# A recurrent transformer and a gated MLP on one core: the last quarter of the first filler chunk moved behind Wo, and row sums spread over two segments

## The chip, the core and the metric

The kernel runs on one core of a Trainium2 chip. The metric is the device time in microseconds; three runs of the kernel before took 1677.53, 1683.88 and 1685.84 us, median 1683.88.

## What is computed

`_A_ref` is a recurrent transformer over 64 segments of 32 rows; each sees 8 memory rows ahead of its own, and the first 8 rows of its output are the memory of the next. `_B_ref` is a gated MLP with a 2048x2048 spatial gate.

```python
def _A_ref(x, mem0, Wq, Wk, Wv, Wo, seg_len):      # Dm 512, 32 heads of 128, M 8, seg 32
    for s in range(n_seg):                         # 64
        h = jnp.concatenate([mem, xs], axis=1)     # 40 rows
        q, k, v = (einsum('btd,dhe->bhte', h, W) for W in (Wq, Wk, Wv))
        p = _softmax(where(mask, q k^T * scale, -1e9))
        o = jnp.einsum('bhte,hed->btd', p v, Wo)
        mem = o[:, :M, :].copy()
        outs.append(o[:, M:, :])
...
def _B_ref(x, w_in, w_sp, b_sp, w_out):            # x 2048x512, w_in 512x1376
    z = _gelu(x w_in);  z1 = z[..., :688];  z2 = _layernorm(z[..., 688:])
    return (z1 * (w_sp z2 + b_sp)) w_out
x = x + _A_ref(_layernorm(x), ...)
x = x + _B_ref(_layernorm(x), ...)
x = x + _A_ref(_layernorm(x), ...)
x = x + _B_ref(_layernorm(x), ...)
```

The sketch writes the einsums of the reference in a short form.

## The kernel before

The program is A, B, A, B: `a_block` (segments), then `b_block` (gMLP), twice. Instructions of TensorE (PE), VectorE (DVE) and ScalarE (ACT) run in the order in which the program writes them (`ORDERED`, `manual_schedule`, L667), in b_block those of SyncE too; around the seam between two blocks a planner still merges the two written orders. GpSimd (POOL) and, in a_block, SyncE are placed by the planner. Each engine works off its queue in order, so an instruction that waits holds up all behind it.

**A segment** (`segment`, L852) takes a little over 10 us. PE projects the 40 rows with Wq, Wk, Wv (groups of four matmuls, one for each 32-row strip of the array, `mm_chunk` L679), computes scores for the two halves r of the heads (`scores`, L899 for the memory part), softmax sums (L921, L930) and the values (`pv`, L938 and L941). ACT scales the scores (L904), DVE adds the mask into E (L907), ACT inverts the sums by Ln and Exp (`memory_out` L955 and L956; all rows L1013 and L1016). DVE writes the normalised heads to uT (L957 for the rows that become memory, L960 and L963 for others). Wo follows in two forms: `wo_pairs` (L755) takes the first `WO_PAIR` heads into the bank px, 2 matmuls of 256 columns a head, `wo_rest` (L762) the others into a strip of psO, 4 matmuls of 128 columns. ACT copies half of px (`odd`, L1011), DVE adds both halves (`fold`, L838), adds psO (memT, L843) and transposes into hT (L844): the memory with which the next segment's first projection (psQ) starts. This is a serial chain through all 64 segments.

**Fillers.** While a segment waits for itself, PE takes pieces of other work by `fill`, which runs a generator to its next `yield`: `b_units` (L718) projects the last 8 rows of each segment of the next 128-row block, six chunks of 16 matmuls, two chunks a segment; `y_part` (L778) applies Wo to such rows of a finished group. The first chunk of a segment was cut into 4, 8 and 4 matmuls: the first 4 before `sums_memory(0)`, the 8 and the last 4 (`fill(2)`) before `sums_memory(1)`; the second chunk, whole, stands behind Wo and covers the memory chain. Both take the PSUM bank accA; px, psm and psV take the bank accB. What ACT does for a chunk is put into `copies` and run at two places (`run(copies)`, which takes the last appended first): behind `memory_out(1)`, ahead of `odd`, and behind the second chunk.

**Row sums.** A finished 128-row block of A's output gets its residual and its layernorm for the gMLP while later segments run. In one segment each, from `tail` to `tail`: loads on SP (`y_load` L204, to tiles y_x and y_o), the sum on POOL (`y_add` L211, in `spare1`), `y_stats` on DVE (bn_stats L134 on 512 columns, in `spare2`, ahead of the fold), the reciprocal root on ACT (`_rstd_act`, Ln L111 and Exp L112, by `copies`), the norm on DVE (`y_norm` L221) and its store. `rows.apply` and `_stats` do the same for the input of later blocks in the first A block.

**The seam.** Behind segment 63 one row (block 11) is finished by hand: its load was issued in segment 63's `spare1` into `rowsB`, the sum is on DVE; then come the last segment's Wo (pw, L1129), its copy (o_end, L1132), two adds on DVE (L1135), stores of them (L1137 on POOL, L1139 on SP) and the load of ACT's gelu table (L106). `b_block` then runs `project(tt)` for 16 row blocks: 16 groups of matmuls into pz (L268, two PSUM buffers), a gelu on ACT (L269), statistics on DVE (L272). Rows 12 to 15 are still due: their loads are on POOL (L205, L207; row 12 in a y_x and a y_o tile, row 15 in a half of wspL), their sums and statistics (`late_sum`) stand behind projects 1, 2 and 3 on DVE, the reciprocal roots on DVE (`norms`), and `late_norm` stores them on POOL. Transposed loads of pairs of row blocks (`load_rows`, L167, on SP) bring them to PE: projects 12 and 13 need rows 12 and 13. Then the gate runs on PE (pg, L369).

Of the kernel before, what the change touches and what calls it, by code (L numbers as in the profile page):

```python
# [8 lines left out]
F32 = mybir.dt.float32  # L9
# [5 lines left out]
P = 128  # L15
DM = 512
# [9 lines left out]
LN_EXP_SET = 6  # L26
GELU_SET = 11
WO_LOW = (4, 4, 4, 3)
WO_PAIR = 14
OLD_SIZES = (H * P, 8 * DH, H * 32, H * 32)  # L30
ORDERED = {mybir.EngineType.PE, mybir.EngineType.DVE, mybir.EngineType.Activation}

# [77 lines left out]
def _rstd_act(nc, out, var, c):  # L110
    nc.scalar.activation(out=out, in_=var, func=ACT.Ln, bias=c["eps_t"][:], scale=1.0)  # L111
    nc.scalar.activation(out=out, in_=out, func=ACT.Exp, scale=-0.5)  # L112
# [19 lines left out]
def _stats(nc, pool, x_tile, MV_out_slot):  # L132
    st = pool.tile([P, nc.vector.BN_STATS_DIM], F32, name="bnst")
    nc.vector.bn_stats(out=st[:], in_=x_tile)  # L134
    nc.vector.bn_aggr(out=MV_out_slot, in_=st[:])


class _Front:
# [496 lines left out]
def a_block(tc, c, rows, front, MV_in, RS_in, MV_out, RS_out, ahead, wo, S, first):  # L635
    nc = tc.nc
    NSEG = S // SEG
    NB = S // P
# [3 lines left out]
    with ExitStack() as ctx:  # L642
# [69 lines left out]
        copies, turns, adds = [], [], []  # L712

        def run(todo):
            while todo:
                todo.pop(0)()

        def b_units(tb, early=False):  # L718
            bs = blk_state[tb]

            for k, j in enumerate((0, 2, 1, 3, 4, 5) if early else (4, 5, 0, 2, 1, 3)):
                ps = (accB if early and k in (1, 3) else accA).tile([P, 512], F32, name="psb")[:]
                for kts in (((0,), (1, 2), (3,)), ((0, 1, 2, 3),))[k % 2]:
                    mm_chunk(ps, lambda kt, cg: bs["hB"][:, kt, :],
                             lambda kt, cg: qk_rhs(w, j, kt, cg) if j < 4 and early else cols_rhs(w, j, kt, cg), kts)
                    if kts[-1] != KT - 1:
                        yield

                def out(k=k, j=j, ps=ps):
                    if j >= 4:  # L730
                        nc.scalar.copy(bs["VB"][:, :, j - 4, :], ps.rearrange("p (i e) -> p i e", i=4))
                        if j == 5 and early:
                            ahead.regroup(bs["VB"], bs["VX"])
                        elif j == 5:
                            store_v(bs)
                        return
                    r = rowsB[:, k % 2, :]
                    nc.scalar.copy(r, ps)
                    t = bs[("QTB", "KTB")[j // 2]][:, j % 2]
                    if early:  # L740
                        turns.append(lambda: nc.vector.transpose(out=t.rearrange("p a b -> p (a b)"), in_=r))
                    else:
                        nc.sync.dma_start_transpose(out=t.rearrange("p (i g) k -> p i (g k)", g=4), in_=r.rearrange("t (i e) -> t i e", i=4))

                copies.append(out)
                yield

        def wo_pairs(px, lhs):  # L750

# [26 lines left out]
        def y_part(G, q, last=False):  # L778

            groups = [oBs[G][:, :, 32 * g:32 * g + 32] for g in range(4)]  # L780
            if last:
                parts = [[(groups[g], 8 * q + k) for g in range(3)] + [(groups[q], 24 + k)] for k in range(8)]
            else:
                parts = [[(groups[g], 8 * q + k) for g in range(4)] for k in range(8)]
            pwB = accA.tile([P, DM], F32, name="pwB")
            for k, _ in enumerate(wo_last(parts, pwB)):
                if k in (0, 2, 3):
                    yield

            def add(lo, n, src):  # L790
                nc.vector.tensor_tensor(out=yB[G][lo:lo + n, :], in0=pwB[src:src + n, :], in1=yB[G][lo:lo + n, :], op=ALU.add)

            def out():
                n = 96 if last else P
                if q == 0:
                    yB[G] = wk.tile([P, DM], F32, name="yB", bufs=1)
                    nc.vector.tensor_copy(yB[G][0:n, :], pwB[0:n, :])
                else:
                    add(0, n, 0)
                if last:  # L800
                    if q == 2:
                        store_last(G, 0, 64, nc.sync)
                    add(32 * q, 32, 96)
                    if q == 2:
                        store_last(G, 64, 96, nc.sync)
                elif q == 3 and G < NB // 4 - 2:
                    stores.append(lambda: store_last(G, 0, P, nc.sync))
                elif q == 3:
                    store_last(G, 0, P, nc.sync)

            adds.append(out)
            yield

        def y_stats(tb):
            rows.y_stats(tb, MV_out[:, tb, :])
            copies.append(lambda: _rstd_act(nc, RS_out[:, tb:tb + 1], MV_out[:, tb, 1:2], c))

        def y_norm(tb, store):
            rows.y_norm(tb, MV_out[:, tb, 0:1], RS_out[:, tb:tb + 1], store)
# [32 lines left out]
        def segment(s, fill, spare1, spare2, tail):  # L852
# [143 lines left out]
            memory_out(0)  # L996
            spare1()
            if not (first and s == 0):
                fill(2)
            sums_memory(1)  # L1000
            pv(1)
            psT = att.tile([P, 2, 512], F32, name="psT")
# [55 lines left out]
        for s in range(NSEG):  # L1058
            tb, j4 = s // 4, s % 4
            if first and s == 0:  # L1060
                more = values(units)
            elif j4 > 0 and tb == NB - 1:
                more = y_part(tb // 4, j4 - 1, last=True)
            elif j4 == (3 if tb < NB - 1 else 0) and tb > 3:
                more = y_part(tb // 4 - 1, tb % 4)
            elif j4 == (first and tb == 0):
                more = b_units(tb + 1)
            if j4 == 1 and tb + 2 < NB:
                rows.load(tb + 2, first, nc.sync)

            def spare1():
                if ys:
                    rows.y_add(ys[0], first, nc.gpsimd, nc.sync)
                elif stores:
                    last = yB[max(yB)][:, 0:1]
                    nc.vector.tensor_copy(last, last)
                    run(stores)
                if j4 == 3 and tb + 2 < NB:
                    rows.apply(tb + 2, MV_in, RS_in, first=first)
                if s == NSEG - 2:  # L1080
                    nc.vector.memset(front.w_in_sb[:, 2, FH - 1:FH + 1], 0.0)
                    front.load_w(2)
                if s == NSEG - 1:
                    nc.vector.memset(rowsB[:, 0, 0:1], 0.0)
                    rows.y_load(due[0], first, nc.sync, rows.pool.tile([P, DM], F32, name="y_x")[:],
                                rowsB[:].rearrange("p a n -> p (a n)").bitcast(F32))()

            def spare2():
                if first and s == 0:
                    rows.apply(1, MV_in, RS_in, first=True)  # L1090
                if first and s == 8:
                    c["cast_bsp"] = c["load_bsp"]()
                if first and s == 12:
                    c["cast_bsp"]()
                if ys:
                    y_stats(ys[0])
                if j4 == 2 and tb + 2 < NB and first:
                    _stats(nc, rows.pool, rows.xs[tb + 2], MV_in[:, tb + 2, :])
                    copies.append(lambda: _rstd_act(nc, RS_in[:, tb + 2:tb + 3], MV_in[:, tb + 2, 1:2], c))

            def tail():
                if j4 == 1 + (first and tb == 0) and tb + 1 < NB:
                    spread_v(blk_state[tb + 1])
                if tb == NB - 1:
                    if j4 != 2:
                        front.load_w(j4)
                    if j4 > 0:
                        front.load_rows(j4 - 1)
                if ys:
                    y_norm(ys.pop(0), nc.sync)  # L1110
                if j4 == 0 and tb > 7 and (tb % 4 == 0 or tb == NB - 1):
                    due.extend(range(tb // 4 * 4 - 8, tb // 4 * 4 - 4) if tb < NB - 1 else range(NB - 8, NB - 4))

                if due and (j4 != 3 or tb + 2 >= NB) and s < NSEG - 1:
                    ys.append(due.pop(0))
                    rows.y_load(ys[0], first, nc.sync)()

            segment(s, lambda n=1: [next(more, None) for _ in range(n)], spare1, spare2, tail)
        assert not ys and due == [NB - 5]
        rows.y_add(due[0], first, nc.vector, nc.sync)  # L1120
        y_stats(due[0])
        run(copies)
        y_norm(due[0], nc.sync)
        ends = (uT[NSEG % 2], oBs[NB // 4 - 1][:, :, 96:128])
        pw = accB.tile([P, 512], F32, name="pw")
        for i in range(H // 2):
# [50 lines left out]
```

## Time and profile before

| what | value |
|---|---|
| median of 3 runs | 1683.88 us |
| the profiled execution | 1684.06 us |
| its span | 1682.4 us |
| PE busy | 1605.9 us, 95% |
| DVE, ACT, POOL busy | 1185.9, 1093.7, 270.3 us |
| granted TensorE clock, mean | 0.996 of full speed |

A line of a timeline gives the start in us, the duration, engine and line, the operation, the tile written and those read, the shapes and the number of instructions put together; in brackets stand the idle time ahead of it on its engine and who ended it. PEld is a weight load of PE, beside its matmuls. POOLq and SPq are DMA issues of those engines. In the waits, a line names the engine, the tile and line that waited, what it waited for, the sum, the number and the longest. All times count from the start of the span.

### The profile page before, as it was taken

The numbers are of one execution on the slowest core, as the hardware profiler recorded it, in microseconds if no ns is written. First come the engines' busy times: TensorE is split into PE (matmuls) and PEld (weight loads), VectorE is DVE, ScalarE is ACT, GpSimd is POOL, SyncE is SP. The second block draws the span as 40 slices with busy tenths as digits, with TensorE's granted clock in tenths as the row PEclk, the third lists the DMA queues.
The fourth block names the chain that finished last, engine by engine and source line by source line (L and its number), as shares of the span: only waits on it lengthen the run. The fifth ranks groups of instructions, "written<-read, shape, count | busy, mean of one in ns | idle before, by whom it ended". The sixth has DMA issues, their size and how long they took to land.

```text
span 1682.4 us, 89162 instructions
## 1 busy us (share of the span) xinstructions
PE 1605.9 (95%) x40146; PEld 934.0 (56%) x40146; DVE 1185.9 (70%) x2848; ACT 1093.7 (65%) x2276; POOL 270.3 (16%) x548
## 2 busy tenths in 40 slices
PE   0999999998999999999999999999999999999999
PEld 0555555554555555556645555555555555655565
DVE  1777777777777787785357777777787778777722
ACT  0677777776777777662037777777777777776500
POOL 5111111111111121220011111111121112112100
PEclk9999999999999999999999999999999999999999
DMA  9222121113312333276972112112252125235697
GB/s 353 90 48 42 41 41 42 42 41 86 73 42 43 81 87 72 68 178 144 196 192 43 44 44 47 49 45 45 51 129 48 44 51 133 56 61 155 144 199 164
DMA packets 270822, 149.45 MB, mean 89 GB/s; under 512 B 199769, under 2 KB 243409, under 8 KB 270441
## 3 DMA queue, kind: packets, MB, share of 16 engines
q1 hardware_dynamic: 262584, 117.23, 31.0%
q0 software_dynamic: 7856, 26.51, 4.7%
q8 instruction: 315, 5.16, 1.3%
q14 instruction: 67, 0.54, 0.1%
HBM read 59.68 MB, written 37.19 MB: 58 GB/s over the span
## 4 chain that ended last, share of the span: by engine, by line
PE 86%; DVE 5%; DMA 5%; ACT 2%; issue 1%; POOL 1%; SPq 0%; DVEq 0%; POOLq 0%; ACTq 0%
PE psQ L679 14%; PE psK L679 13%; PE psb L679 10%; PE psO L762 6%; PE psm L679 6%; PE pg L369 6%; PE px L755 6%; PE psV L679 6%; PE pz L268 4%; PE pwB L774 3%; PE psO L921 2%; PE psO L938 2%; PE psT L930 2%; PE py L412 2%; PE psS L895 1%; DMA Wk_sb<-in_A_Wk_dram 1%
## 5 line engine op out<-in xcount | busy, mean ns | idle before, releaser
L679 PEld LDWEIGHTS <-hT 128*32 128x32 bf16 x12288 | 313.5, 97 | 353.1 <-DVE hT L844 71.4
L872 DVE STREAM_TRANSPOSE QQ<-rows 128x512 bf16<-128x512 bf16 x256 | 181.0, 707 | 28.4 <-ACT rows L869 22.2
L872 DVE STREAM_TRANSPOSE KA<-rows 128x512 bf16<-128x512 bf16 x256 | 179.8, 702 | 27.5 <-ACT rows L869 21.1
L869 ACT CAST rows<-psQ 128x512 bf16<-128x512 f32 x256 | 148.1, 587 | 45.4 <-PE psQ L679 45.2
L957 DVE TENSOR_TENSOR uT<-psO,Rm 128x128 bf16<-128x128 f32 x256 | 74.5, 291 | 137.0 <-ACT Rm L956 136.1
L679 PE MATMUL psQ<-Wq_sb,hT 128*32 128x512 bf16 x2048 | 136.2, 385 | 21.3 <-DVE hT L844 15.2
L960 DVE TENSOR_TENSOR uT<-psO,Rt 128x384 bf16<-128x384 f32 x256 | 141.0, 551 | 20.3 <-ACT Rt L1016 16.7
L369 PE MATMUL pg<-z,wspT 128*128 128x344 bf16 x1024 | 154.4, 309 | 0.0
L762 PE MATMUL psO<-Wo_high,uT 128*32 128x128 bf16 x8704 | 148.6, 220 | 2.4 <-issue 2.1
L1016 ACT ACTIVATE Rt<-Rt 128x512 f32<-128x512 f32 x256 | 147.2, 622 | 4.1
L762 PEld LDWEIGHTS <-uT 128*32 128x32 bf16 x9216 | 143.8, 97 | 5.6 <-issue 4.4
L904 ACT ACTIVATE S<-psS 128x224 bf16<-128x224 f32 x256 | 91.4, 357 | 80.8 <-PE psS L899 80.8
L679 PE MATMUL psQ<-Wk_sb,hT 128*32 128x512 bf16 x2048 | 134.8, 382 | 0.0
L679 PE MATMUL psm<-Wq_sb,hT 128*32 128x512 bf16 x2048 | 134.2, 381 | 0.0
L679 PE MATMUL psK<-Wk_sb,hT 128*32 128x512 bf16 x2048 | 133.6, 379 | 0.0
L679 PE MATMUL psK<-Wv_sb,hT 128*32 128x512 bf16 x2048 | 133.4, 379 | 0.0
L1013 ACT ACTIVATE Rt<-psT 128x1024 f32<-128x1024 f32 x128 | 131.0, 1023 | 3.1
L679 PE MATMUL psV<-Wv_sb,hT 128*32 128x512 bf16 x2048 | 132.8, 378 | 0.0
L369 PEld LDWEIGHTS <-wspT 128*128 128x128 bf16 x1024 | 100.1, 98 | 53.4 <-DMA wspT<-in_B_w_sp_dram 0.3
L955 ACT ACTIVATE Rm<-psO 128x128 f32<-128x128 f32 x256 | 71.0, 277 | 84.4 <-PE psO L941 70.8
L755 PE MATMUL px<-Wo,uT 128*32 128x256 bf16 x3584 | 121.7, 275 | 0.5 <-DVE uT L957 0.5
L831 POOL COPY KX<-front 128x128 bf16<-128x128 bf16 x128 | 68.3, 550 | 321.1 <-PE psS L899 249.3
(171 smaller groups left out, 2758.4 us busy)
## 6 DMA issues: line engine op xcount, KB each, us to landing
o_d<-o_sb SPq DMA_DIRECT2D x126, 64.0 KB
vb_d<-front SPq DMA_DIRECT2D x30, 256.0 KB
VX<-vb_d SPq DMA_DIRECT2D x120, 64.0 KB
ln_x<-xd SPq DMA_DIRECT2D x26, 256.0 KB
y_o<-o_d SPq DMA_DIRECT2D x22, 256.0 KB
xd<-y_o SPq DMA_DIRECT2D x22, 256.0 KB
y_x<-xd SPq DMA_DIRECT2D x22, 256.0 KB
Wq_sb<-in_A_Wq_dram POOLq DMA_DIRECT2D x8, 512.0 KB, 9.2
```

The costliest lines, as they stand in the source:

```text
L369: nc.tensor.matmul(pg[t][:, k, 0:344], lhsT=wsp[t][:, st, :], rhs=z(st, 344 * k, 344 * k + 344), start=(st == 0), stop=(st == NT - 1))
L679: return [nc.tensor.matmul(ps[32 * cg:32 * cg + 32, :], lhsT=lhs(kt, cg), rhs=rhs(kt, cg), start=(kt == 0), stop=(kt == KT - 1), tile_posi ...
L755: nc.tensor.matmul(px[at:at + 32, 0:256], lhsT=lhs[:, h, :], rhs=wo_rhs(h, slice(k, 4, 2)), start=(h < 2), stop=(h >= WO_PAIR - 2), tile_p ...
L762: nc.tensor.matmul(pw[32 * cg:32 * cg + 32, :], lhsT=lhs[:, h, :], rhs=wo_rhs(h, cg), start=False, stop=(h == H - 1), tile_position=(0, 32 ...
L869: return r, mms, nc.scalar.copy(r[:], ps)
L872: nc.vector.transpose(out=QQ[:, j % 2, :, 0:32] if j < 2 else KA[:, j % 2], in_=r[:])
L904: return nc.scalar.activation(out=S[:, r], in_=psS[:, r, 0:224], func=ACT.Exp, scale=scale)
L955: nc.scalar.activation(out=rm, in_=psO[r][:, :, 320:384], func=ACT.Ln)
L957: nc.vector.tensor_tensor(out=hview(uT_cur[:], r, 24, 32), in0=oview(r, 0, 8), in1=rm.rearrange("p g (n q) -> p g n q", q=8), op=ALU.mult)
L960: nc.vector.tensor_tensor(out=hview(uT_nxt[:], r, 0, 24), in0=oview(r, 8, 32), in1=rview(r, 0, 24), op=ALU.mult)
L1013: nc.scalar.activation(out=Rt[:], in_=psT[:], func=ACT.Ln)
L1016: nc.scalar.activation(out=rt, in_=rt, func=ACT.Exp, scale=-1.0)
```

## The change

Two heads of Wo move from `wo_pairs` to `wo_rest` (14 to 12). The last quarter of a segment's first filler chunk (in `y_part` likewise) moves from before `sums_memory(1)` to behind Wo, ahead of the second chunk; the second chunk takes accB, px's bank; the first chunk's copy is no longer ahead of `odd`, and both copies run behind the second chunk. A row sum takes two segments: load in the `tail` of one, the sum on POOL in the next one's `spare1`, statistics in two halves of 256 columns in `spare1` and `spare2` of the one after it, norm and the next load in its `tail`. The input's statistics of the first A block are halved in the same way. In the last segments a load may be issued for row 11 into `rowsB`, in segment 63's `tail`, so that behind the loop rows 10 and 11 both get statistics, reciprocal roots and norms, where only row 11 did.

```diff
-WO_PAIR = 14
+WO_PAIR = 12
...
+def _half_stats(nc, st, x_tile, k, MV_out_slot):
+
+    nc.vector.bn_stats(out=st[:, k, :], in_=x_tile[:, 256 * k:256 * k + 256])
+    if k:
+        nc.vector.bn_aggr(out=MV_out_slot, in_=st[:])
...
-                ps = (accB if early and k in (1, 3) else accA).tile([P, 512], F32, name="psb")[:]
+                ps = (accB if k % 2 else accA).tile([P, 512], F32, name="psb")[:]
...
-                        elif j == 5:
+                        elif j == 4 and not early:
                             store_v(bs)
...
-                copies.append(out)
-                yield
+                if early or k % 2 == 0:
+                    copies.append(out)
+                else:
+                    copies.insert(0, out)
+                if early or k % 2:
+                    yield
...
-                if k in (0, 2, 3):
+                if k in (0, 2):
                     yield
...
-        def y_stats(tb):
-            rows.y_stats(tb, MV_out[:, tb, :])
-            copies.append(lambda: _rstd_act(nc, RS_out[:, tb:tb + 1], MV_out[:, tb, 1:2], c))
+        def y_stats(tb, k):
+
+            if k == 0:
+                halves[tb] = rows.pool.tile([P, 2, nc.vector.BN_STATS_DIM], F32, name="bnst2")
+            _half_stats(nc, halves[tb], rows.y[tb][0], k, MV_out[:, tb, :])
+            if k:
+                copies.append(lambda: _rstd_act(nc, RS_out[:, tb:tb + 1], MV_out[:, tb, 1:2], c))
...
             if not (first and s == 0):
-                fill(2)
+                fill()
...
             def spare1():
-                if ys:
-                    rows.y_add(ys[0], first, nc.gpsimd, nc.sync)
-                elif stores:
+                for y, added in ys:
+                    if added:
+                        y_stats(y, 0)
+                    else:
+                        rows.y_add(y, first, nc.gpsimd, nc.sync)
+                if stores and not ys:
...
-                if s == NSEG - 1:
-                    nc.vector.memset(rowsB[:, 0, 0:1], 0.0)
-                    rows.y_load(due[0], first, nc.sync, rows.pool.tile([P, DM], F32, name="y_x")[:],
-                                rowsB[:].rearrange("p a n -> p (a n)").bitcast(F32))()
...
-                if ys:
-                    y_stats(ys[0])
...
+                for y, added in ys:
+                    if added:
+                        y_stats(y, 1)
...
-                if ys:
-                    y_norm(ys.pop(0), nc.sync)
+                if ys and ys[0][1]:
+                    y_norm(ys.pop(0)[0], nc.sync)
+                for y in ys:
+                    y[1] = True
...
-                if due and (j4 != 3 or tb + 2 >= NB) and s < NSEG - 1:
-                    ys.append(due.pop(0))
-                    rows.y_load(ys[0], first, nc.sync)()
+                if due and (not ys or tb == NB - 1):
+                    y = due.pop(0)
+                    ys.append([y, False])
+                    if tb == NB - 1 and y % 2:
+                        nc.vector.memset(rowsB[:, 0, 0:1], 0.0)
+                        rows.y_load(y, first, nc.sync, rows.pool.tile([P, DM], F32, name="y_x")[:],
+                                    rowsB[:].rearrange("p a n -> p (a n)").bitcast(F32))()
+                    else:
+                        rows.y_load(y, first, nc.sync, rows.pool.tile([P, DM], F32, name="y_x")[:], rows.pool.tile([P, DM], F32, name="y_o")[:])()
...
-        rows.y_add(due[0], first, nc.vector, nc.sync)
-        y_stats(due[0])
+        rows.y_add(NB - 5, first, nc.vector, nc.sync)
+        for y, _ in ys:
+            for k in range(2):
+                y_stats(y, k)
         run(copies)
-        y_norm(due[0], nc.sync)
+        for y, _ in ys:
+            y_norm(y, nc.sync)
```

More of the change, by code (lines that the diff above doesn't have):

```diff
@@ L812, in y_part, with x_stats @@
             yield
-        def y_stats(tb):
-            rows.y_stats(tb, MV_out[:, tb, :])
-            copies.append(lambda: _rstd_act(nc, RS_out[:, tb:tb + 1], MV_out[:, tb, 1:2], c))
+        halves = {}
+        def y_stats(tb, k):
[4 more added lines that the diff above has]
+                copies.append(lambda: _rstd_act(nc, RS_out[:, tb:tb + 1], MV_out[:, tb, 1:2], c))
+        def x_stats(tb, k):
+            if k == 0:
+                halves["x"] = rows.pool.tile([P, 2, nc.vector.BN_STATS_DIM], F32, name="bnst3")
+            _half_stats(nc, halves["x"], rows.xs[tb], k, MV_in[:, tb, :])
+            if k:
+                copies.append(lambda: _rstd_act(nc, RS_in[:, tb:tb + 1], MV_in[:, tb, 1:2], c))
         def y_norm(tb, store):
@@ L1067, in a_block @@
                 more = b_units(tb + 1)
-            if j4 == 1 and tb + 2 < NB:
+            if j4 == 0 and tb + 2 < NB:
                 rows.load(tb + 2, first, nc.sync)
             def spare1():
-                if ys:
-                    rows.y_add(ys[0], first, nc.gpsimd, nc.sync)
-                elif stores:
+                for y, added in ys:
[4 more added lines that the diff above has]
+                if stores and not ys:
                     last = yB[max(yB)][:, 0:1]
@@ L1077, in spare1 @@
                     run(stores)
+                if first and j4 == 1 and tb + 2 < NB:
+                    x_stats(tb + 2, 0)
                 if j4 == 3 and tb + 2 < NB:
@@ L1094, in spare2 @@
                     c["cast_bsp"]()
-                if ys:
-                    y_stats(ys[0])
-                if j4 == 2 and tb + 2 < NB and first:
-                    _stats(nc, rows.pool, rows.xs[tb + 2], MV_in[:, tb + 2, :])
-                    copies.append(lambda: _rstd_act(nc, RS_in[:, tb + 2:tb + 3], MV_in[:, tb + 2, 1:2], c))
+                for y, added in ys:
+                    if added:
+                        y_stats(y, 1)
+                if first and j4 == 1 and tb + 2 < NB:
+                    x_stats(tb + 2, 1)
             def tail():
@@ L1108, in tail @@
                         front.load_rows(j4 - 1)
-                if ys:
-                    y_norm(ys.pop(0), nc.sync)
+                if ys and ys[0][1]:
+                    y_norm(ys.pop(0)[0], nc.sync)
+                for y in ys:
+                    y[1] = True
                 if j4 == 0 and tb > 7 and (tb % 4 == 0 or tb == NB - 1):
                     due.extend(range(tb // 4 * 4 - 8, tb // 4 * 4 - 4) if tb < NB - 1 else range(NB - 8, NB - 4))
-                if due and (j4 != 3 or tb + 2 >= NB) and s < NSEG - 1:
-                    ys.append(due.pop(0))
-                    rows.y_load(ys[0], first, nc.sync)()
-            segment(s, lambda n=1: [next(more, None) for _ in range(n)], spare1, spare2, tail)
-        assert not ys and due == [NB - 5]
-        rows.y_add(due[0], first, nc.vector, nc.sync)
-        y_stats(due[0])
+                if due and (not ys or tb == NB - 1):
[7 more added lines that the diff above has]
+                        rows.y_load(y, first, nc.sync, rows.pool.tile([P, DM], F32, name="y_x")[:], rows.pool.tile([P, DM], F32, name="y_o")[:])()
+            segment(s, lambda n=1: [next(more, None) for _ in range(n)], spare1, spare2, tail)
+        assert not due and ys == [[NB - 6, True], [NB - 5, False]]
+        rows.y_add(NB - 5, first, nc.vector, nc.sync)
+        for y, _ in ys:
+            for k in range(2):
+                y_stats(y, k)
         run(copies)
-        y_norm(due[0], nc.sync)
+        for y, _ in ys:
+            y_norm(y, nc.sync)
         ends = (uT[NSEG % 2], oBs[NB // 4 - 1][:, :, 96:128])
```

## The prediction

> **What bounds the kernel now.** I read the page first: TensorE is busy 95% of the span, and the chain of work that ended last is 86% PE.
>
> ```profile
> PE 1605.9 (95%) x40146; PEld 934.0 (56%) x40146; DVE 1185.9 (70%) x2848; ACT 1093.7 (65%) x2276; POOL 270.3 (16%) x548
> ...
> PE 86%; DVE 5%; DMA 5%; ACT 2%; issue 1%; POOL 1%; SPq 0%; DVEq 0%; POOLq 0%; ACTq 0%
> ```
>
> So only PE's idle time counts; the waits tell where it is: `PEld L679 <- DVE hT L844` has 71.4 us in 125 waits, the longest 4.8. That is each segment's first projection waiting for the memory that the segment before it made. The timeline of a quiet segment (25) shows the chain: Wo (L755, L762), odd copy, fold, memT, transpose, psQ.
>
> ```profile
> 315.47 0.95 PE L755 MATMUL px<-Wo,uT 128*32 128x256 bf16 x28
> 315.84 0.57 ACT L738 CAST rowsB<-psb 128x512 bf16<-128x512 f32 x1
> 316.47 0.37 ACT L1011 COPY odd<-px 64x256 f32<-64x256 f32 x1
> 316.87 0.58 DVE L838 TENSOR_TENSOR t<-px,odd 64x128 f32<-64x128 f32 x2 [0.62 <-ACT odd L1011]
> 317.25 1.04 PE L679 MATMUL psb<-Wk_sb,hB 128*32 128x512 bf16 x16
> 317.55 0.29 DVE L843 TENSOR_TENSOR memT<-psO,t 128x128 bf16<-128x128 f32 x1
> 317.88 0.31 DVE L844 STREAM_TRANSPOSE hT<-memT 128x128 bf16<-128x128 bf16 x1
> ```
>
> The filler (psb, 16 matmuls) covers the chain, not quite: psQ's first matmul starts at 318.24, 0.34 after psb's last. Groups of four matmuls follow each other every 0.216 us, and between two groups with no wait the same distance is 0.205. Over the 111 segments with a filler and no large stall, the distance above 0.205 sums to 15.6 us.
>
> Some segments stand far longer. In segment 34 DVE waits for POOL's row sum, which waits for a load, and the fold is queued on DVE behind the statistics:
>
> ```profile
> 411.89 1.15 POOL L211 TENSOR_TENSOR y_o<-y_o,y_x 128x512 f32<-128x512 f32 x1 [13.02 <-DMA y_o<-o_d]
> 413.07 0.69 DVE L134 BATCH_NORM_STATS2 bnst<-y_o 128x6 f32<-128x512 f32 x1 [3.23 <-POOL y_o L211]
> 414.85 0.55 DVE L838 TENSOR_TENSOR t<-px,odd 64x128 f32<-64x128 f32 x2
> 416.19 1.90 PE L679 MATMUL psQ<-Wq_sb,hT 128*32 128x512 bf16 x16 [4.32 <-DVE hT L844]
> ```
>
> Seven such segments have periods of 14.66, 13.09, 11.45, 11.34, 11.43, 10.82 and 11.50 against 10.31: 12.1 us over, and 13.1 with the normal gap that the 15.6 does not count there.
>
> The third place is the end of an A block, where gMLP's projections begin (first block; the second is alike):
>
> ```profile
> 727.67 0.68 DVE L211 TENSOR_TENSOR rowsB<-rowsB,y_x 128x512 f32<-128x512 f32 x1
> 728.80 9.47 PE L268 MATMUL pz<-front 128*128 128x512 bf16 x48
> 729.77 0.57 ACT L1132 COPY o_end<-pw 128x512 f32<-128x512 f32 x1
> 730.35 1.28 ACT L106 ACT_TABLE_LOAD   x1
> 730.54 1.40 DVE L1135 TENSOR_TENSOR o_end<-pw,o_end 32x512 f32<-32x512 f32 x2
> 731.65 1.32 ACT L269 ACTIVATE z<-pz 128x1376 bf16<-128x1376 f32 x1
> 737.55 0.54 POOL L207 DMA_DIRECT2D wspL<-o_d  x1 [4.44 <-DMA o_d<-o_end]
> ```
>
> One table load, hidden under pz; a projection takes 2.34 us (37.44 for 16), a gelu 1.32, and PE never waits.
>
> **The change, part by part.** Sums are against the profiled execution: 1684.06 us, of which 1682.4 is the span. It lies 0.2 above the median of 1683.88.
>
> (a) *Filler shift.* Four of the first chunk's matmuls move behind Wo. Ahead of psQ stand then five groups of four: 5 x 0.216 + 0.045 = 1.12 us. The chain needs 1.04 (eight segments without filler show that from Wo's last matmul to psQ), 1.10 behind statistics. So the whole 15.6 goes: **-15.6**. What it exposes: the second psO's sums (L921) wait for E of that half (L907, 0.39), which the moved quarter helped to cover; two groups remain and leave about 0.08 us. Where POOL copies lengthen E to 0.49 to 1.32 us, in a few segments, it shows: summed over them **+1.2**. The first chunk's copy (L738, 0.57) now stands behind the exps, not ahead of odd; two copies there, 0.47 apart, still end before psQ's own copy.
>
> The second chunk goes to accB, the bank of px, and must wait until the fold has read px. With 24 px matmuls and no copy ahead, odd starts 0.1 earlier and the fold ends 1.87 us after px began; the chunk starts 2.01 after. Margin 0.07 to 0.14: cost nothing.
>
> (b) *WO_PAIR 12.* Two heads move from px to psO. Per head px takes 0.77/14 = 0.055 us and psO 1.01/18 = 0.056: +0.00 to 0.02 a segment, **+1** taken for 128.
>
> (c) *Row sums over two segments.* A sum now has a segment between load and add, another between add and statistics; half statistics of 256 columns cost about 0.40 (0.69 for 512, 0.50 for 344). One half stands ahead of the fold where DVE idles 0.62 for odd. Segment 34's 13.02 on POOL shows that a load can take over one segment; POOL would then be late, but no longer DVE. **-13.1**; bounds -7.1 (only the two largest stalls go) and -13.7 (their segments fall to 10.2 too).
>
> (d) *End of segment 63.* pw waits 0.91 for uT; the copies leave ACT's path to it: **-0.6** for both blocks.
>
> (e) *End of the block.* Here two rows, 10 and 11, are finished behind the loop. Row 11's load is issued in segment 63's tail, a segment later than before, and DVE's add waits for it. Statistics of both rows come behind that add, so their rstds (Ln 0.29, Exp 0.20) are ready when gelu has begun. In the built order of the changed kernel ACT runs, after row 9's Ln and Exp: table, gelu 0, table, Ln 10, table, gelu 1, table, Exp 10, table, Ln 11, table, gelu 2, table, Exp 11, o_end's copy, table, gelu 3. That is eight loads where one was: 18 in the program instead of 4. The first waits with gelu 0 for pz 0. From pz 0's end (731.3): 1.28 + 1.32 = gelu 0 to 733.97; gelu 1 to 738.2; gelu 2 to 743.9; o_end's copy at 745.4; gelu 3 to 748.6. Before, gelu 3 ended at 739.6. PE has two pz buffers, so pz 5 starts at 748.65, not 740.4: **+8.25 a block at the least**.
>
> A second chain is later still. The last pz pairs need rows 12 to 15, which pass through adds and statistics on DVE. Row 12's y_o tile is that of row 10, so its load waits for row 10's norm, behind Exp 10 (740.3). The page's DMA part gives such a load 5.5:
>
> ```profile
> wspL<-o_d POOLq DMA_DIRECT2D x4, 256.0 KB, 4.1
> ...
> y_o<-o_d POOLq DMA_DIRECT2D x2, 256.0 KB, 5.5
> ```
>
> So add 12 at 745.9, statistics to 747.3, norm 11, then the o_end adds at 749.3, before at 730.5. Their store and row 15's load, queued on POOL behind it, follow: 4.9 to 6.7 for the store and 4.1 for the load; add 15 ends some 16.1 late. Then one rstd on DVE (2.45), four norms, a store (3 us) and the transpose, queued last on SP: 751.0 before, 767.1 to 769.3 now, landing by 770.3 to 772.5. pz 12 started at 756.8, so +13.6 a block (13.5 to 15.7), which includes the 8.25; gates (L369) are bound by PE and take nothing back. PE then idles up to 4 us, and an idle stretch has a price of its own, as behind segment 34's stall:
>
> ```profile
> 411.90:416.20 4.30, 0.01 (x4) 0.01 (x4) 2.88 (x9) 2.22 (x7) 1.53 (x2) 0.84 0.41 124
> 416.20:418.00 1.80, 1.80 (x20) 0.73 (x24) 1.80 (x6) 0.00 (x0) 0.40 (x1) 0.50 0.07 18
> 420.00:422.40 2.40, 2.40 (x36) 1.02 (x32) 0.94 (x2) 1.01 (x2) 0.52 (x2) 0.66 0.39 109
> ```
>
> Windows of 34 (window, length, busy by engine, granted clock): after 4.3 idle the clock is 0.50, then 0.66. That cost 2.8 us; idles of 1.0 to 1.5 us show no drop. I take 1 a block of the 0 to 2.8: **2 x (13.6 + 1) = +29.2**, bounds 16.5 and 36. The Trainium skill (TensorE: Matmul & The Clock Gate, "Part 1: The HAM clock gate") halves the clock after about one 3.4 us window of idleness; segment 34 agrees. By it the floor case alone, whose longest idle is 3.35, would cost nothing more, and the second chain's idle 2.8.
>
> **Sum.** 1684.06 - 15.6 + 1.2 + 1 - 13.1 - 0.6 + 29.2 = 1686.2: **1686**.
>
> **Rivals.**
> 1. *Only ACT's floor counts*: rows 12 to 15 are ready in time (their loads land earlier than the DMA medians), so 16.5 instead of 29.2: 1673.5. For it: the waits of POOL overlap; against it: the tile of row 10 and DVE's order are fixed in the program.
> 2. *The far side: the second chunk waits in accB.* If the fold ends later than the 0.07 us margin, psQ slips in each of 111 segments: 11 us per 0.1. From 0.13 us late the kernel is slower than before by over 0.5%; at 0.21 the whole gain is gone: 1702. For it: the half bn_stats ahead of the fold and a margin of hundredths of a us; against it: odd loses the copy ahead of it.
> 3. *The spread doesn't do what it says*: POOL adds wait still longer and statistics still wait: +13.1, 1699. For it, the 13.02; against it, a whole segment of 10.3 more.
> 4. *A switch costs more than the load.* The row: o_end's copy ends 730.34, load from 730.35 to 731.63, gelu at 731.65: no more than 0.02 beyond 1.28. A drain behind each load as long as the load would add 7 x 1.3 x 2 = 18: 1704. The Trainium skill (ScalarE: Activation LUTs, "What ACT_TABLE_LOAD costs") gives about 1.38 us of drain besides a load of 1.28; by it the sum would be 19 more. The row here speaks against the drain.
> 5. *Everything at the boundary is hidden*: -29: 1657. Only if the loads are not in the executed stream.
>
> **How the numbers follow.** The measurement can tell about 0.5% (8.4 us) from no change: faster is under 1675.5, slower over 1692.3. Forecast 0.50, its own range 1676 to 1697 (0.04 below 1675.5, 0.40 between, 0.06 above); rival 1 0.17, rival 5 0.05, rival 2 0.12, rival 3 0.09, rival 4 0.07. Faster 0.04 + 0.17 + 0.05 = 0.26, same 0.40, slower 0.06 + 0.28 = 0.34. The range 1671 to 1701 leaves out rivals 4 and 5 and half of 2, 0.18.
>
> **What would show it.** (a): distance to psQ 0.205, periods 10.2 in quiet segments; wrong if psb in accB waits for the fold (L838). (b): 24 and 80 matmuls in 1.78 us. (c): no period over 10.6; wrong if bn_stats still wait for POOL. (e): eight table loads a block, pz 5 8 us and pz 12 about 14 us later after pz 0 than before; wrong if the late rows' transpose lands before pz 11 ends, or the clock stays at 1.00. Above all the sum stands or falls with (e): it alone turns a gain of 27 us into nothing.

## The result and the profile after

The changed kernel took 1694.32 us (median of 6 runs, 1690.16 to 1696.62); the kernel before 1681.63 (6 runs, 1677.53 to 1685.84). The ratio is 1.007, 95% interval 1.0047 to 1.0094: slower by some 12.7 us, and the whole interval lies above 1. The profiled execution has a span of 1693.8 us, 11.4 more than before.

Three lines of the page: the busy time; the DMA queue that brings PE's instructions (packets, MB, share); and the chain that ended last:

```profile
PE 1598.1 (94%) x40658; PEld 981.1 (58%) x40658; DVE 1187.3 (70%) x2888; ACT 1108.8 (65%) x2290; POOL 264.3 (16%) x548
...
q8 instruction: 319, 5.23, 1.3%
...
PE 85%; DVE 4%; DMA 4%; ACT 3%; issue 3%; POOL 1%; SPq 0%; POOLq 0%; DVEq 0%; ACTq 0%
```

PE has 512 instructions more and is busy 7.8 us less, in a span that is longer. "Issue", time in which an engine waited for nothing that the profile shows, went from 1% to 3% of the chain, and no step of the prediction has a price for it.

Segment 30 of the second block is a quiet one and answers to segment 25 of before:

```profile
1190.20 0.84 PE L764 MATMUL px<-Wo,uT 128*32 128x256 bf16 x24
1191.09 0.37 ACT L1034 COPY odd<-px 64x256 f32<-64x256 f32 x1 [0.43 <-PE px L764]
1191.49 0.58 DVE L861 TENSOR_TENSOR t<-px,odd 64x128 f32<-64x128 f32 x2 [0.51 <-ACT odd L1034]
1191.98 0.39 PE L686 MATMUL psb<-Wq_sb,hB 128*32 128x512 bf16 x4
1192.20 1.04 PE L686 MATMUL psb<-Wk_sb,hB 128*32 128x512 bf16 x16
1192.54 0.31 DVE L867 STREAM_TRANSPOSE hT<-memT 128x128 bf16<-128x128 bf16 x1
1193.06 0.39 PE L686 MATMUL psQ<-Wq_sb,hT 128*32 128x512 bf16 x4
```

hT is done at 1192.85 and psQ starts at 1193.06, when PE comes to it: the chain is covered. Segment 34, where DVE had stood behind POOL, has its statistics in two halves and a fold on time:

```profile
409.38 0.42 DVE L140 BATCH_NORM_STATS2 bnst<-y_o 128x6 f32<-128x256 f32 x1
410.29 0.42 DVE L140 BATCH_NORM_STATS2 bnst<-y_o 128x6 f32<-128x256 f32 x1
410.88 0.58 DVE L861 TENSOR_TENSOR t<-px,odd 64x128 f32<-64x128 f32 x2
412.49 0.39 PE L686 MATMUL psQ<-Wq_sb,hT 128*32 128x512 bf16 x4
```

The seam of the first block:

```profile
721.33 0.38 SPq L214 DMA_DIRECT2D rowsB<-o_d  x1
721.71 4.82 PE L275 MATMUL pz<-front 128*128 128x512 bf16 x24
724.28 1.28 ACT L276 ACT_TABLE_LOAD   x1 [6.04 <-PE pz L275]
725.49 0.69 DVE L218 TENSOR_TENSOR rowsB<-rowsB,y_x 128x512 f32<-128x512 f32 x1 [4.70 <-DMA rowsB<-o_d]
725.57 1.32 ACT L276 ACTIVATE z<-pz 128x1376 bf16<-128x1376 f32 x1
726.91 1.28 ACT L111 ACT_TABLE_LOAD   x1
728.20 0.29 ACT L111 ACTIVATE RS<-MV,eps_t 128x1 f32<-128x1 f32 x1
728.51 1.28 ACT L276 ACT_TABLE_LOAD   x1
736.93 4.03 PE L275 MATMUL pz<-front,ln_x 128*128 128x512 bf16 x12 [3.27 <-ACT z L276]
740.18 2.53 ACT L276 ACTIVATE z<-pz 128x1376 bf16<-128x1376 f32 x2
741.54 2.48 PE L275 MATMUL pz<-front,ln_x 128*128 128x512 bf16 x12 [0.59 <-ACT z L276]
```

Tables alternate as forecast; pz 5 starts at 741.54, 19.83 behind pz 0 (forecast 19.85). From pz 0 to the gate it takes 46.4 us in the first block and 48.8 in the second, before 37.3 and 37.2.

And the new thing, in the middle of Wo in segment 55 of the second block:

```profile
1451.81 0.22 PE L771 MATMUL psO<-Wo_high,uT 128*32 128x128 bf16 x1
1453.08 0.17 PEld L771 LDWEIGHTS <-uT 128*32 128x32 bf16 x11 [1.23 <-issue]
1453.08 0.35 PE L771 MATMUL psO<-Wo_high,uT 128*32 128x128 bf16 x11 [1.05 <-issue]
1453.48 0.29 DVE L866 TENSOR_TENSOR memT<-psO,t 128x128 bf16<-128x128 f32 x1 [1.41 <-PE psO L771]
```

PE waits 1.23 us for nobody, in its own weight loads, and the memory chain (memT) waits with it. The two traces, cut into segments, show many: a pause is the time by which an instruction starts later than the median at its place of the segment. I counted PE's instructions (a weight load and its matmul are two): nearly all these pauses stand at one and the same place of the count modulo 256. The page's instruction queue brings 5.23 MB in 319 packets of 16 KB, and PE has 2 x 40,658 instructions and 338 of its queue, that is 256 for each packet. In the packets' own records each such pause over 0.1 us of the changed kernel ends 1.2 to 1.6 us after a packet ended, 2.2 to 3.4 us after it began. So PE had used up a packet before the next was there. The sum of these pauses is 8.1 us before and 22.5 after.

Where the 11.4 us of the span come from, in us:

| place | forecast | measured |
|---|---|---|
| gap ahead of psQ, quiet segments | -15.6 | -15.5 |
| stalls behind statistics | -13.1 | -13.3 |
| waits for E | +1.2 | +3.3 |
| px and psO without pauses | +1 | -0.3 |
| pauses where a packet of instructions ends | none | +14.4 |
| seam, projections 0 to 15, both blocks | +29.2 | +9.0 and +11.6 |
| start, to the first psQ (44.7, then 47.8) | none | +3.1 |
| the rest (between blocks, gates, end) | -0.6 | -0.9 |

The start is spent waiting for weights and lies between 44.6 and 48.6 in the runs below, without order.

### The profile page after: what moved, and what is told of

Same layout as the page of the kernel before. It is cut to its first block, busy times and chain, and to the rows that moved or that the text cites. A ratio compares the mean times of both kernels' runs of the same rounds, so it can differ in the third digit from the quotient of the medians.

```text
span 1693.8 us, 90162 instructions
## 1 busy us (share of the span) xinstructions
PE 1598.1 (94%) x40658; PEld 981.1 (58%) x40658; DVE 1187.3 (70%) x2888; ACT 1108.8 (65%) x2290; POOL 264.3 (16%) x548
## 3 DMA queue, kind: packets, MB, share of 16 engines
q8 instruction: 319, 5.23, 1.3%
## 4 chain that ended last, share of the span: by engine, by line
PE 85%; DVE 4%; DMA 4%; ACT 3%; issue 3%; POOL 1%; SPq 0%; POOLq 0%; DVEq 0%; ACTq 0%
PE psQ L686 13%; PE psK L686 12%; PE psb L686 10%; PE pg L376 8%; PE psO L771 8%; PE psm L686 6%; PE px L764 6%; PE psV L686 5%; PE pwB L783 3%; PE psO L944 2%; PE py L419 2%; PE pz L275 2%; PE psT L953 2%; PE psO L961 2%; PE psS L918 1%
## 5 line engine op out<-in xcount | busy, mean ns | idle before, releaser
L686 PEld LDWEIGHTS <-hT 128*32 128x32 bf16 x12288 | 352.2, 97 | 283.6 <-DVE hT L867 23.6
L771 PEld LDWEIGHTS <-uT 128*32 128x32 bf16 x10240 | 157.7, 97 | 15.8 <-issue 15.0
L892 ACT CAST rows<-psQ 128x512 bf16<-128x512 f32 x256 | 144.1, 594 | 34.5 <-PE psQ L686 34.0
L854 POOL COPY KX<-old 128x128 bf16<-128x128 bf16 x128 | 67.3, 528 | 431.0 <-PE psS L922 227.1
L686 PE MATMUL psb<-Wq_sb,hB 128*32 128x512 bf16 x992 | 89.2, 389 | 41.5 <-POOL hB L609 41.5
```

What stands on the lines that cost most here:

```text
L686: return [nc.tensor.matmul(ps[32 * cg:32 * cg + 32, :], lhsT=lhs(kt, cg), rhs=rhs(kt, cg), start=(kt == 0), stop=(kt == KT - 1), tile_posi ...
L771: nc.tensor.matmul(pw[32 * cg:32 * cg + 32, :], lhsT=lhs[:, h, :], rhs=wo_rhs(h, cg), start=False, stop=(h == H - 1), tile_position=(0, 32 ...
L854: nc.gpsimd.tensor_copy(KX[:, :, r].rearrange("p g (k i) -> p i g k", i=4), bs["KTB"][:, r].rearrange("p (i g) k -> p i g k", i=4)[:, :, : ...
L892: return r, mms, nc.scalar.copy(r[:], ps)
```

## The experiments

Each ratio is to the kernel before, run again beside the versions; its medians there are 1682.16 (runs 1 to 4), 1679.40 (5 to 8) and 1680.53 us (9 and 10).

**1. The seam mended.** Row 10 is finished first, row 11 behind the last Wo's copy and adds, its root on DVE.

```diff
-        rows.y_add(NB - 5, first, nc.vector, nc.sync)
-        for y, _ in ys:
-            for k in range(2):
-                y_stats(y, k)
+        for k in range(2):
+            y_stats(NB - 6, k)
         run(copies)
-        for y, _ in ys:
-            y_norm(y, nc.sync)
+        y_norm(NB - 6, nc.sync)
...
-        run(copies)
+        rows.y_add(NB - 5, first, nc.vector, nc.sync)
+        for k in range(2):
+            y_stats(NB - 5, k)
+        copies.clear()
+        _rstd_dve(nc, wk, RS_out[:, NB - 5:NB - 4], MV_out[:, NB - 5, 1:2], 1)
+        y_norm(NB - 5, nc.sync)
```

> The changed kernel, with only the end of the A block rewritten: row 10 gets its statistics, root (ACT) and norm first, then come the last Wo's copy and adds, and row 11's sum, statistics and norm behind them, its root on DVE. ACT then has one table load at each seam, ahead of which Ln and Exp of row 10 stand. Theory (the seam's loss is ACT's table loads and what they hold up; 9.0 and 11.6 us in the two blocks): 1694.3 - 20.7 = 1673.6, 1672 to 1677, projections 0 to 15 back in 37.3 us. Rival (rows 12 to 15 are late by themselves, because row 11's load is late and POOL's load for row 12 waits behind it): 1 to 6 us a block stay at projection 12: 1676 to 1686. Rival (the loss is not the seam's): 1694. In the segments nothing changes: pauses at every 256th instruction of PE sum to about 22 us, as in the changed kernel.

Measured: 1674.02 us, ratio 0.9948 (0.9929 to 0.9967). Projections 0 to 15 took 38.2 and 39.3 us; pauses 17.2. The seam was the loss; 0.8 us stay in the first block (PE waits 0.94 at projection 6) and 2.2 in the second (1.99 at projection 12), so the second rival has a small part.

**2. The filler alone.** The kernel before with the diff's filler, bank and 12 heads, and its own row sums.

> The kernel before, with the filler's shift, the second chunk in accB and 12 heads in pairs, and the row sums and the seam as before. Theory (PE's instructions come in packets of 256; with the slow quarter taken out from ahead of sums and Wo, and 8 more small matmuls in Wo, a packet is used up before the next is there, in 35 to 40 segments for 0.3 to 1.3 us): psQ's gap is 0.205, which gives 15.6 back, pauses go from 8 to about 22 us and waits for E cost about 3: 1681.6 - 15.6 + 14.4 + 3 = 1683, 1680 to 1686, not faster. Rival (the pauses come of the spread row sums and their DMA traffic): pauses stay at 8, 1681.6 - 15.6 + 3 = 1669. The bn_stats stalls (13.1) stay in both.

Measured: 1690.74, ratio 1.005 (1.0033 to 1.0068); pauses 17.6. The rival falls: the pauses come with the filler and its 12 heads, not with the row sums. The median is 8 above the theory's 1683, but the profiled execution, the fastest of eight, took 1684.62, so the trace can't show where these 8 come from. It does show something else; segment 34 again:

```profile
410.19 1.16 POOL L211 TENSOR_TENSOR y_o<-y_o,y_x 128x512 f32<-128x512 f32 x1 [12.46 <-DMA y_o<-o_d]
411.38 0.69 DVE L134 BATCH_NORM_STATS2 bnst<-y_o 128x6 f32<-128x512 f32 x1 [2.85 <-POOL y_o L211]
413.75 1.05 PE L679 MATMUL psb<-Wk_sb,hB 128*32 128x512 bf16 x16 [3.83 <-DVE t L842]
```

The second chunk is in accB and waits 3.83 us for the fold, so it no longer runs during the stall but behind it. PE's matmuls wait for the fold in 3 places in this run, 8.6 us in all (18 further waits, of some 0.28 us each, are of weight loads alone). The changed kernel has none, because there the fold is never late.

**3. The spread alone**, with the mended seam; fillers, banks and 14 heads as before.

> The kernel before with the row sums over two segments, and the mended seam of the other run; fillers, banks and the 14 heads in pairs as before. Theory (the spread takes the seven stalls away and has no price of its own): 1681.6 - 13.1 = 1668.5, 1666 to 1672, pauses at 256 instructions about 8 us as before, psQ's gap 0.34 again. Rival (the spread makes the pauses): 22 us of pauses, 1683.

Measured: 1671.19, ratio 0.9937 (0.9921 to 0.9953); pauses 6.5; the distance to psQ is 0.34 again and sums to 14.1 us over 0.205. The spread is worth what was forecast, and it has no price in pauses.

**4. Mended seam, 14 heads** (`WO_PAIR = 14`). Beside run 3 it differs only by the filler's shift and its bank.

> The changed kernel with the mended seam and 14 heads in pairs: 4 matmuls (8 instructions) fewer a segment, px 0.11 us longer. Theory (pauses are fetches that come late for dense instructions): 8 instructions fewer in the dense stretch lengthen a packet by about 0.2 us, pauses fall from 22 to about 15 us; against that the fold ends 0.11 later, within or just beyond the margin of 0.07 to 0.14, 0 to 5 us: 1666 to 1673, faster than the run with 12 by 2 to 7. Rival (pauses are set by DMA traffic and not by PE's instructions): as with 12 heads or slower by the fold, 1673 to 1679.

Measured: 1669.67, ratio 0.9920 (0.9903 to 0.9936); pauses 11.7. The fold ended 1.98 after px began and the second chunk started at 2.04, not 2.00: it waits 0.04. Beside run 3 the gap ahead of psQ is gone (14.1 us), but pauses rise from 6.5 to 11.7, and over all segments the two traces differ by 2.2 us only; what takes the other few us was not separated. The two ratios can't be told apart, so the shift is not shown to gain anything by itself.

**5. The kernel before with 12 heads** (`WO_PAIR = 12`, nothing else).

> The kernel before with nothing changed but 12 heads in pairs for 14: 4 matmuls (8 instructions) more a segment, all in Wo. Theory (PE's packets of 256 instructions come late where instructions are dense): packets that are used up faster than in 3.4 us become more, pauses go from 8 to 11 to 14 us, the Wo time itself moves by no more than 0.02 a segment: 1684 to 1688, slower by 3 to 6. Rival (the number of Wo's instructions doesn't matter, the rate per head is the same): within 1 us of before, 1681 to 1683, pauses 8.

Measured: 1687.51 beside 1679.4 of before, ratio 1.0042 (1.0027 to 1.0058). Slower, as the theory said, but its pauses are only 10.5: 2.4 of some 8 us, less than a third. In its trace, which is of the slowest of nine executions (1691.13), waits for E have grown by 3.2 and the large stalls behind statistics by some 6; whether 8 more instructions a segment bring these about, or they vary from run to run, stays open.

**6. Mended seam, 16 heads** (`WO_PAIR = 16`).

> The changed kernel with the mended seam and 16 heads in pairs. px is 0.11 us longer than with 14, so the fold ends 2.09 after px began and the second chunk, in the fold's bank, waits for it: 0.11 a segment more than with 14, in 118 segments 13 us. This is the mechanism of rival 2 of the prediction, brought about on purpose: 11 us for each 0.1. Against it 8 dense instructions fewer a segment and a wait that lets the fetch come in time: pauses from 12 to about 6. Theory (bank wait): 1669.7 + 13 - 6 = 1677, 1674 to 1681, psQ's gap still 0.205 and the gap ahead of the second chunk 0.15 longer. Rival (only the fetch counts): 1664.

Measured: 1676.44, ratio 0.9979 (0.9964 to 0.9993); pauses 4.5. A segment of it:

```profile
277.16 0.58 DVE L861 TENSOR_TENSOR t<-px,odd 64x128 f32<-64x128 f32 x2 [0.15 <-ACT odd L1034]
277.43 0.39 PE L686 MATMUL psb<-Wq_sb,hB 128*32 128x512 bf16 x4
277.79 0.55 PEld L686 LDWEIGHTS <-hB 128*32 128x32 bf16 x16 [0.32 <-DVE t L861]
```

The second chunk waits for the fold: it starts 2.145 after px, 0.11 later than with 14 heads, which reckons to 13 us over 118 segments; in the two traces all segments together are 3.5 us longer with 7.2 us of pauses less, 10.7 in all. This is the price that rival 2 named, and the fewest pauses do not pay for it.

**7. Half a packet's shift.** As run 4, with 64 unread matmuls at the start:

```diff
+                for _ in range(16 if early and k == 0 else 0):
+                    for cg in range(4):
+                        nc.tensor.matmul(ps[32 * cg:32 * cg + 32, :], lhsT=bs["hB"][:, 0, :], rhs=qk_rhs(w, j, 0, cg), start=True, stop=True, tile_position=(0, 32 * cg))
```

> As the run with the mended seam and 14 heads, with 64 matmuls more at the very start of the program, whose result nobody reads: all later instructions of PE shift by 128, half a packet, and nothing else changes. Theory (a pause stands where a packet of 256 ends): the pauses leave the segments where they were (59, 104, 113 and 121, counted over both blocks, had the largest, 0.72 to 1.27 us) and come in segments out of 4, 8, 12, 14, 18, 24, 26, 27, 29, 32, 35, 40, 43, 44, 46, 49, 52, 57, 60, 61, 69, 70, 73, 76, 77, 80, 88, 89, 91, 94, 97, 105, 106, 108, 111, 114, 122, 123, 125, still at one place of the count modulo 256; their sum stays between 9 and 15 us and the time between 1667 and 1674. Rival (pauses belong to segments, by their DMA traffic or waits): the same segments as before.

Measured: 1672.77, ratio 0.9958 (0.9939 to 0.9978); pauses 12.7. Of the 25 segments that pause over 0.1 us not one is among the 25 of run 4; 15 of them were on the list. All 25 hold the end of a packet that by run 4's trace, shifted by 128 instructions and without pauses, is used up in under 3.4 us, as 52 of the 128 segments do (the ten that the list left out: 3.13 to 3.35). The pauses belong to the count of instructions, not to segments.

**8. Mended seam, 13 heads** (`WO_PAIR = 13`).

> The changed kernel with the mended seam and 13 heads in pairs. Theory: the fold ends 1.93 after px began, the second chunk no longer waits for it (with 14 it waited 0.04 a segment, 5 us in all), but 4 instructions more a segment make the pauses 3 us longer: 1669.7 - 5 + 3 = 1668, 1665 to 1671, a tie with 14 within what can be measured. Rival (the bank's wait with 14 is hidden behind hT): 1672, between 14 and 12.

Measured: 1670.79, ratio 0.9941 (0.9923 to 0.9960); pauses 11.2. It can't be told from 14. The fold ended 1.965 after px, not 1.93, and the chunk's wait is nearly the same (2.027): the step with an odd number of heads was mis-sized.

**9. The changed kernel with row 11 loaded earlier**, into two tiles that are free by then, and nothing else:

```diff
+                if s == NSEG - 1:
+                    rows.y_load(due[0], first, nc.sync, *(a[1].rearrange("p r h k -> p (r h k)").bitcast(F32) for a in (KTBr, QTBr)))()
...
-                    if tb == NB - 1 and y % 2:
+                    if s == NSEG - 1:
+                        pass
+                    elif tb == NB - 1 and y % 2:
```

> The changed kernel with one thing altered: row 11's two loads are issued in segment 63's first spare place, as before the change, into two tiles of the last segments that are free by then, and not in its tail into rowsB behind row 9's norm. Order of the code, 12 heads in pairs, fillers and all else as in the changed kernel. Theory (the seam's loss hangs on this load alone: it makes DVE's sum, so the roots, so ACT's tables late): one table load a seam, projections 0 to 15 in 37.2 to 37.4 us in both blocks, 20 us back: ratio to before 0.993 to 0.996, some 1672 to 1675. Rival (two rows behind the loop are too many whatever the load): late rows still hold projection 12 by 1 to 4 us a block: 1676 to 1680. Rival (tables go on switching): 1692. Pauses of PE as in the changed kernel, 17 to 22 us.

Measured: 1671.80, ratio 0.9944 (0.9930 to 0.9958); pauses 18.4. Its seam:

```profile
718.17 0.68 DVE L218 TENSOR_TENSOR old<-old,old 128x512 f32<-128x512 f32 x1
720.12 0.20 ACT L112 ACTIVATE RS<-RS 128x1 f32<-128x1 f32 x1
721.15 0.20 ACT L112 ACTIVATE RS<-RS 128x1 f32<-128x1 f32 x1
721.85 1.28 ACT L106 ACT_TABLE_LOAD   x1
```

One table load. The sum no longer waits for a transfer, and both roots come ahead of gelu. Projections took 37.9 and 41.0 us, so 16.3 of the 22 us that are back lie in the seams; in the two traces pauses are 4.1 and the start is 2.5 less, and these vary between runs. The 3.8 that stay in the second block are not at projection 12, where the rival had them, but at projection 2:

```profile
1534.67 0.55 DVE L228 TENSOR_SCALAR ln_xn<-old,MV,RS 128x512 bf16<-128x512 f32 x1 [2.24 <-DMA xb_d<-ln_xn]
1535.25 1.40 DVE L1173 TENSOR_TENSOR o_end<-pw,o_end 32x512 f32<-32x512 f32 x2
1535.97 2.52 ACT L276 ACTIVATE z<-pz 128x1376 bf16<-128x1376 f32 x2 [1.61 <-DVE o_end L1173]
1537.33 2.90 PE L275 MATMUL pz<-front 128*128 128x512 bf16 x10 [1.98 <-ACT z L276]
```

Row 11's norm waits for a buffer that a store still reads, the last Wo's adds stand behind it on DVE, gelu 0 waits for them, and PE for gelu 0. The granted clock was then 0.50 from 1539.5 to 1541.5, after an idle stretch of about 2 us.

**10. The same with 14 heads.**

> The same with 14 heads in pairs, the version that the runs so far point to. Theory: the mended seam of the other run with 14 heads still lost 0 and 3.7 us at projection 12, since row 12's load waits on POOL for row 11's sum; with the early load that goes too, so 2 to 4 us under the run with the mended seam and 14 heads (ratio 0.992): ratio 0.989 to 0.991, 1663 to 1667, pauses 9 to 13 us. Rival (what held projection 12 there is the DMA traffic at that point): 0.992 again.

Measured: 1666.87, ratio 0.9926 (0.9909 to 0.9942); pauses 9.5; projections 37.9 and 39.4 us, the wait at projection 2 again (2.35 in the second block). So the early load gains nothing over run 4, and it can't be told from it: what it saves at projections 6 and 12 it loses at 2. These two, 0.992 and 0.993, have the lowest ratios and are faster than both kernels, but runs 3, 8 and 9 (0.994) can't be told from them, and run 3 has the old fillers: what is shown to gain is the spread with a seam that doesn't lose.

The pauses beside the packets that would, without pauses, be used up in under 3.4 us:

| kernel | pauses, us | packets under 3.4 us |
|---|---|---|
| before | 8.1 | 39 |
| spread alone, 14 heads | 6.5 | 41 |
| mended seam, 16 heads | 4.5 | 44 |
| mended seam, 14 heads; early load | 11.7; 9.5 | 62; 60 |
| before with 12 heads | 10.5 | 66 |
| filler alone, 12 heads | 17.6 | 83 |
| changed; mended seam; early load (12 heads) | 22.5; 17.2; 18.4 | 83; 82; 83 |

In the changed kernel no packet whose own time was 3.5 us or more pauses by over 0.1 us; of those under 3.4 about half do. The counts of packets shift by some ten to fifteen with the instruction that a packet is taken to begin with. The last row shows how far pauses vary between runs whose segments have one order of instructions.

## Why the prediction held, and where it was wrong

The time lies in the range, within the forecast's own 1676 to 1697, but the forecast's middle case (within 0.5%) did not come: the kernel is slower, by 0.7%. That the time lies in the range is in part luck: two terms failed in opposite directions, 14.4 us of pauses that had no term and a seam that cost 8.6 less than forecast.

- **(a) Filler shift.** Right for the gap ahead of psQ: 15.5 of 15.6, and the fold's margin in accB held (126 ns measured, forecast 70 to 140). Rival 2 did not happen in the changed kernel; runs 2 and 6 show that it is real and its price about right: 0.11 a segment cost some 11 to 13 us. But the step gave the moved quarter no price in instructions: with 14 heads the shift raises the pauses from 6.5 (run 3) to 11.7 (run 4).
- **E's wait** was mis-sized: 3.3 for 1.2. POOL's row sum (1.27) falls on E, as here, where E takes 1.21 and not 0.39. In the changed kernel a row sum stretches eight Es to 0.85 to 1.48 us; before, two (0.64 and 1.32):

```profile
1261.24 1.27 POOL L218 TENSOR_TENSOR y_o<-y_o,y_x 128x512 f32<-128x512 f32 x1 [9.40 <-PE psS L922]
1261.55 1.21 DVE L930 TENSOR_TENSOR E<-S,maskN 128x448 bf16<-128x448 bf16 x1
1262.82 0.23 PE L944 MATMUL psO<-E,ones 64*128 64x64 bf16 x4 [0.67 <-DVE E L930]
```

- **(b) 12 heads, "+1".** The rate per head was right (-0.3 measured). The step that failed, here and in (a), is to price moved work by its rate alone. Taking the quarter, 8 slow instructions, from ahead of Wo and putting 8 more into Wo (16 more for psO, 8 fewer for px) makes packets short, and 14.4 us of pauses is what the change really pays; two heads raise them from 11.7 (run 4) to 17.2 (run 1). It could have been seen: before's waits list PEld L762 with 4.4 us of "issue", and its two longest pauses in a Wo are 0.66 and 0.59 us.
- **(c) Spread.** Right: 13.3, and run 3 alone; no bn_stats waits for POOL any more. The sign "no period over 10.6" failed all the same, since pauses and waits for E make segments of up to 12.25 us.
- **(e) Seam.** The mechanism and the floor were right to hundredths; the second chain was mis-sized, 20.7 for 29.2. Row 12's load took 3.2 us from issue to its sum, not the 5.5 of the DMA part; o_end's store let row 15's load go after 3.7, not 4.9 to 6.7; that load took 3.6 in the second block, not 4.1. So rows 12 to 15 cost 0.8 and 3.4 beyond the floor, not 5.35: rival 1 was nearly the case. The median of two transfers, from a busier moment, was the wrong row.
- **The clock** did fall, and its price was hidden:

```profile
733.66:736.93 3.27, 0.00 (x1) 0.00 (x1) 0.24 (x1) 3.21 (x5) 0.39 (x1) 0.96 0.76 200
736.93:740.96 4.03, 4.03 (x12) 1.56 (x12) 3.58 (x8) 3.99 (x5) 1.08 (x2) 0.61 0.26 98
```

After 3.27 us of idleness the granted clock was 0.61, and one projection took 4.03, not 2.48; but gelu 3 ended only at 741.5, so PE waited anyway. In the second block it was 0.50 for 3.71 us after as long an idle stretch, and pz 5 took 2.90, before 2.32; further on PE waited 2.57 for the transposed load of rows 12 and 13. The rule that the prediction cited from the Trainium skill (TensorE: Matmul & The Clock Gate, "Part 1: The HAM clock gate") gives an idle window of about 3.4 us; here 3.27 sufficed, and in run 9 about 2, so the prediction's reading of it, that 3.35 would cost nothing, was wrong about the clock and nearly right about the sum.
- **Rival 4**, a drain behind each table load: none. The load at 724.28 ends at 725.56 and gelu starts at 725.57. The 2.66 us a switch of the Trainium skill (ScalarE: Activation LUTs, "What ACT_TABLE_LOAD costs") is 1.28 here.

## What to carry to other kernels

When small matmuls are packed closer, count instructions as well as time: work that is off the data's critical path may have been what gave the instruction stream its time. A load issued one step later can cost far more than its length when an engine with two function tables stands behind it; look at the built order of that engine and count the table loads. Take a transfer's time from a row at the same place, not from a median of few.

## What the runs showed of the hardware

In the changed kernel PE's instructions came in 319 packets of 16 KB, 256 instructions each, most of them 3 to 6 us apart. Where PE paused, it went on 2.2 to 3.4 us after the last packet's transfer began; a transfer took 0.9 to 2.0. Where 256 instructions were used up in under 3.4 us PE could stop, for up to 1.3 us (1.9 in run 8), in the middle of a run of matmuls that waited for no other engine. Why the fetch begins when it does was not tried.
